# A top-32 attention with two mixtures on one core: which weight piece GpSimd subtracts, and when token and output transposes run

## The chip, the core and the metric

The kernel runs on one core of a Trainium2 chip, on TensorE (matmuls), VectorE, ScalarE, GpSimd and SyncE, each with a queue of its own that is worked off in order. SyncE's queue (SP) issues the loads, GpSimd's queue also issues the indirect transfers of the outputs. The metric is the device time of one execution in microseconds (us), the median of three runs.

## What is computed

Eight heads of attention in which each query keeps its 32 highest scores, then a dense layer with Mish, then a mixture of eight experts, of which each token takes the one with the highest cosine. The change lies in that last part:

```python
for e in range(E):                      # E = 8, D = 512, F = 1024, 1152 tokens
    mask = expert_idx == e
    h = np.maximum(x[mask] @ w1[e], 0.0)
    out[mask] = gate_w[mask, None] * (h @ w2[e])
```

## The kernel before

The attention and the dense layer come first, in an order that a planner in the file works out; the change doesn't touch it. The second mixture follows, from about 534 us to the end, in an order that is written out by hand as a loop over 64 steps (and three more): step f = 0 to 7 of expert e = 0 to 7. Tokens were sorted by expert into DRAM (`xs`), up to 176 for each expert.

All matmuls of this part are made in two parts, a high part in a shorter float format and a low part, which is the rest. So each piece of weights is split: `split_piece` (L1203) lets ScalarE copy the raw piece to the high part (L1209), and later GpSimd or VectorE subtracts the high part from the raw piece to get the low part (L1177, in the helper `low`). Which of them does it is set by the piece's number modulo 8: those in `POOL_LO` go to GpSimd, the others to VectorE. Pieces of even number are of `w1`, of odd number of `w2`, four each for an expert. Step f of expert e splits piece f of expert e + 1. There are three raw tiles of 512 KB; when a piece is subtracted, its raw tile is loaded with the piece that comes three later (`load_piece`, on SP).

A step f of expert e makes, in this order on TensorE:

- `hidden` (L1302): `phe`, the product of the tokens with 128 columns of `w1`. ScalarE and VectorE turn it into `hs` (L1315), the positive part `ht`, and its low part (L1317).
- at two of the steps, `tokens` (L1277): 4 transposes of the next expert's tokens into the one bank `pxe`/`po`, from which ScalarE (copy) and VectorE (L1177) make `xt`.
- `outputs` (L1320): the product of an earlier `ht` (three steps back) with `w2`, added up in four PSUM banks `py` 0 to 3.
- at two of the steps, `scatter` (L1355): 4 transposes of the finished outputs `yT` of the expert before into the same bank `po`; ScalarE scales them to `yo` (L1364), and GpSimd sends them out (L1365).

The outputs of expert e − 1 are finished in step 2 of expert e, and those of e begin in step 3, in the same four banks. Between the two lies `gather` (L1348): for each of the four banks ScalarE copies one half to `yT` (L1352) and VectorE adds the other half (L1353). A bank is free for the next expert when its addition is done.

Work that follows a matmul isn't put into the queues at once: `later(dt, ...)` holds it until TensorE's planned time has gone on by dt. So the order on ScalarE, VectorE, GpSimd and SP comes from the order of the steps and from these delays.

`load_tokens` loads the tokens of the expert after next (`xe`, one tile) at step 5. For the last expert (e = 7) there are no tokens to prepare, and `scatter` runs at steps 3 and 4.

Of the kernel before, what the change touches and what calls it, by code (L numbers as in the profile page):

```python
# [25 lines left out]
NE = 8  # L26
# [26 lines left out]
NRAW = 3  # L53
NIDLE = 56
NTAIL = 3
POOL_LO = (2, 5)
PE, ACT, DVE, POOL, SP = range(5)

WINDOW = 3.4133
# [255 lines left out]
def sparse_attention_mish_moe_kernel(  # L315
# [34 lines left out]
    def tp_bank(name):  # L350
        return psum.tile([P, 512], F32, tag="tp", name=name, bufs=TP[0])
# [815 lines left out]
    def later(dt, f, *a):  # L1167
        heapq.heappush(events, (clk[0] + dt, next(serial), f, a))

    def pe(dt):  # L1170
        clk[0] += dt
        while events and events[0][0] <= clk[0]:
            _, _, f, a = heapq.heappop(events)
            f(*a)
# [28 lines left out]
    def split_piece(i):  # L1203
# [5 lines left out]
        nc.scalar.activation(t[:, 0:1024], raw, AF.Copy)  # L1209
        eng = nc.gpsimd if i % 8 in POOL_LO else nc.vector  # L1210

# [9 lines left out]
    def pieces(n):  # L1221

        for _ in range(n):
            if loaded[1] < loaded[0]:
                split_piece(loaded[1])
                loaded[1] += 1
# [45 lines left out]
    def load_tokens(e):  # L1272
        xe = m2.tile([CH, 2, W], F32, tag="xe", name=f"xe{e}", bufs=1)
        nc.sync.dma_start(xe, xs[e * CAP:(e + 1) * CAP, :].rearrange("(c p) w -> p c w", p=CH))
        XE[e] = xe

    def tokens(e, d):  # L1277

        xe = XE[e]
        if d == 0:  # L1280
            XT2[e] = m2.tile([P, 4, C2], F32R, tag="xt", name=f"xt{e}", bufs=2)
            IG[e] = m2.tile([CH, 2, 2], F32, tag="ig", name=f"ig{e}", bufs=4)
            nc.gpsimd.tensor_copy(IG[e].bitcast(I32), xe[:, :, DM:W].bitcast(I32))
        xt = XT2[e]
        if e == 0 and d == 0:
            pt = psum.tile([P, 512], F32, tag="h", name=f"pxe{e}{d}", bufs=3)
        else:
            pt = tp_bank(f"pxe{e}{d}")
        for c in range(2):
            for j in range(2):  # L1290
                nc.tensor.transpose(
                    pt[:, (2 * c + j) * CH:(2 * c + j + 1) * CH],
                    xe[:, j, (2 * d + c) * P:(2 * d + c + 1) * P],
                    ident[0:CH, 0:CH],
                )
        pe(0.44)
        p3 = pt[:, 0:C2].rearrange("p (c t) -> p c t", c=2)
        hi = xt[:, 2 * d:2 * d + 2, 0:CAP]
        later(0.2, nc.scalar.activation, hi, p3, AF.Copy)
        later(0.8, low, xt[:, 2 * d:2 * d + 2, CAP:C2], p3, hi, nc.vector)  # L1300

    def hidden(e, f):  # L1302
        ph = psum.tile([P, 512], F32, tag="h", name=f"phe{e}_{f}", bufs=3)
        w = W1[e][:, f // 2].rearrange("p (l c f) -> p l c f", l=2, c=4)[:, :, :, f % 2 * P:f % 2 * P + P]
        x = XT2[e]
        for c in range(4):
            nc.tensor.matmul(ph[:, 0:C2], w[:, 0, c], x[:, c, :], start=(c == 0), stop=False)  # L1307
        for c in range(4):
            nc.tensor.matmul(ph[:, 0:CAP], w[:, 1, c], x[:, c, 0:CAP], start=False, stop=(c == 3))
        pe(1.02)  # L1310
        hs = m2.tile([P, CAP], F32, tag="hs", name=f"hs{e}_{f}", bufs=3)
        ht = m2.tile([P, C2], F32R, tag="ht", name=f"ht{e}_{f}", bufs=5)
        HT[e, f] = ht
        later(L2[0], nc.scalar.activation, hs, ph[:, CAP:C2], AF.Copy)
        later(L2[1], lambda: nc.vector.tensor_tensor(hs, hs, ph[:, 0:CAP], op=ALU.add))  # L1315
        later(L2[2], nc.scalar.activation, ht[:, 0:CAP], hs, AF.Relu)
        later(L2[3], lambda: nc.vector.scalar_tensor_tensor(  # L1317
            ht[:, CAP:C2], hs, 0.0, ht[:, 0:CAP].bitcast(F32), op0=ALU.max, op1=ALU.subtract))

    def outputs(e, f):  # L1320
        if f == 0:
            PY[e] = [psum.tile([P, 512], F32, tag=f"y{d}", name=f"py{e}_{d}", bufs=1) for d in range(4)]
        w = W2[e][:, f // 2].rearrange("p (l c d) -> p l c d", l=2, c=2)[:, :, f % 2]
        ht = HT.pop((e, f))
        for d in range(4):
            nc.tensor.matmul(PY[e][d][:, 0:C2], w[:, 0, d * P:(d + 1) * P], ht, start=(f == 0), stop=False)  # L1326
            nc.tensor.matmul(PY[e][d][:, 0:CAP], w[:, 1, d * P:(d + 1) * P], ht[:, 0:CAP], start=False, stop=(f == 7))  # L1327
            pe(0.255)
            if f == 7:
                later(0.2, gather, e, d)  # L1330

    def last_outputs(f, j):

        e = NE - 1
        if f == 0:
            PY[e, j] = psum.tile([P, 512], F32, tag=f"y{j}", name=f"py{e}_{j}", bufs=1)
        w = W2[e][:, f // 2].rearrange("p (l c d) -> p l c d", l=2, c=2)[:, :, f % 2]
        ht = HT[e, f] if j == 0 else HT.pop((e, f))
        t = slice(j * CH, j * CH + CH)
        for n, (a, l) in enumerate(((ht[:, t], 0), (ht[:, t], 1), (ht[:, CAP + j * CH:CAP + j * CH + CH], 0))):  # L1340
            nc.tensor.matmul(PY[e, j][0:CH], a, w[:, l], start=(f == 0 and n == 0), stop=(f == 7 and n == 2))
        pe(0.64)
        if f == 7:
            later(0.2, write, e, j, PY[e, j])
# [10 lines left out]
    def scatter(e, j):  # L1355
        po = tp_bank(f"po{e}{j}")
        for c in range(4):
            nc.tensor.transpose(po[0:CH, c * P:(c + 1) * P], YT[e][:, c, j * CH:(j + 1) * CH], ident)
        pe(0.44)
        later(0.2, write, e, j, po)  # L1360
# [18 lines left out]
    for g in range(8 * NE + 3):  # L1379
        e, f = g // 8, g % 8  # L1380
        if g < 8 * NE:
            hidden(e, f)
            pieces(1)
        if f in (3, 4) and e < NE - 1:
            tokens(e + 1, f - 3)
        if f == 5 and e < NE - 2:
            load_tokens(e + 2)
        if 3 <= g < 8 * NE - 5:
            outputs((g - 3) // 8, (g - 3) % 8)
        elif g >= 8 * NE - 5:  # L1390
            f_ = g - 8 * NE + 5
            last_outputs(f_, 0)
            if f_ < 8 - NTAIL:
                last_outputs(f_, 1)
        if 0 < e < NE and 0 <= f - (5 if e < NE - 1 else 3) < 2:
            scatter(e - 1, f - (5 if e < NE - 1 else 3))
    for f in range(8 - NTAIL, 8):
        last_outputs(f, 1)
    while events:
# [275 lines left out]
```

## Time and profile before

| | |
|---|---|
| three runs | 716.85, 720.65, 729.57 us, median 720.65 us |
| profiled execution | 718.75 us, of which the span from first to last instruction 717.0 us |
| busy over the span | TensorE 92%, VectorE 72%, ScalarE 71%, GpSimd 46% |
| mean granted clock of TensorE | 0.969 of full speed |
| chain that ended last, shares | TensorE 50%, transfers 15%, VectorE 14%, ScalarE 9% |

How to read the rows of the next section but one. Engines are PE (TensorE matmuls), PEld (its weight loads), DVE (VectorE), ACT (ScalarE), POOL (GpSimd), SP (SyncE). In a row of the timeline stand: start in us from the span's start, duration in us, engine, line, operation, output<-inputs, sizes and count; behind it in brackets the idle time ahead of the instruction and what ended it, where that is more than some 0.15 us. A row may hold several like instructions (x3, x4). In a row of the busy time by stretches stand: the stretch and its length, then busy us and count of PE, PEld, DVE, ACT and POOL, then the granted clock of TensorE (1.00 is full speed), the share of DMA time and GB/s. In a row of the waits: who waited, for what, us in total, how often, the longest.

### The profile page before, as it was taken

To read this page: it belongs to the slowest core of one execution; us is meant where nothing else is said; L and a number is where in the kernel's file an instruction comes from. 1 tells how busy PE (TensorE), PEld (TensorE's weight loads), DVE (VectorE), ACT (ScalarE), POOL (GpSimd) and SP (SyncE) were. 2 spreads that over 40 slices of the span, in tenths; PEclk is the share of its full clock that TensorE was granted. 3 is DMA by queue.
4 is the path that set the end of the run, shared out by engine and by line. 5 is a ranking of instruction groups with operands and counts; after the bars stand their busy time and mean duration, and the time that the engine had idled before them with its cause. 6 is when DMAs were issued, how large, how long until landed. Compare 5 with 4: busy or idle time off the path is not lost.

```text
span 717.0 us, 14819 instructions
## 1 busy us (share of the span) xinstructions
PE 659.4 (92%) x5244; PEld 500.8 (70%) x5244; DVE 519.3 (72%) x2044; ACT 506.5 (71%) x1084; POOL 332.0 (46%) x319
## 2 busy tenths in 40 slices
PE   7878788988999999999999999999989898998895
PEld 5545565655687666767667767686579898998893
DVE  4999989999987888798697783141228787778741
ACT  4868788888698877875887875773326677667651
POOL 4677786766463666344255552820013323333321
PEclk9999987999999999999999999999989999999998
DMA  9924434310012010011000001520026677777600
GB/s 257 293 93 134 146 118 142 128 43 16 30 34 49 2 32 2 3 36 39 1 1 1 31 2 60 177 88 0 0 72 224 195 229 231 226 231 225 211 24 23
DMA packets 57738, 68.98 MB, mean 96 GB/s; under 512 B 22958, under 2 KB 41390, under 8 KB 57656
## 3 DMA queue, kind: packets, MB, share of 16 engines
q1 hardware_dynamic: 55656, 63.23, 29.2%
q0 software_dynamic: 2000, 4.73, 1.9%
q8 instruction: 43, 0.70, 0.4%
q14 instruction: 39, 0.32, 0.2%
HBM read 60.32 MB, written 8.15 MB: 95 GB/s over the span
## 4 chain that ended last, share of the span: by engine, by line
PE 50%; DMA 15%; DVE 14%; ACT 9%; issue 7%; POOL 3%; POOLq 0%; SPq 0%; ACTq 0%; DVEq 0%
PE px L1054 15%; PE ph L994 12%; DMA raw<-in_moe_w_dram 8%; PE pv L885 5%; PE pt L834 4%; PE ps L673 4%; DMA out_dram<-yo,ig 2%; DVE cand L714 2%; DVE t L767 2%; PE pv L880 2%; ACT w L1209 2%; DVE w_out_s L418 1%; PE phe L1307 1%; DMA raw<-in_moe_w_in_dram 1%; ACT e L750 1%
## 5 line engine op out<-in xcount | busy, mean ns | idle before, releaser
L1054 PE MATMUL px<-w_out_s,g 128*128 128x512 f32 x288 | 142.9, 612 | 0.0
L994 PE MATMUL ph<-xT,w_in_h 128*128 128x256 f32 x576 | 90.5, 297 | 0.8 <-DVE g L1044 0.8
L1177 POOL TENSOR_TENSOR w<-raw,w 128x1024 fp32r<-128x1024 f32 x22 | 53.2, 2425 | 78.9 <-ACT w L1209 60.1
L714 DVE MAX8 cand<-sp 128x8 f32<-128x72 f32 x576 | 82.9, 217 | 2.4 <-ACT sp L441 2.3
L994 PEld LDWEIGHTS ph<-xT,w_in_h 128*128 128x128 f32 x576 | 75.0, 191 | 12.4 <-issue 5.2
L759 POOL TENSOR_SCALAR e<-sp,t 128x576 f32<-128x576 f32 x37 | 66.3, 1791 | 32.2 <-ACT e L750 26.7
L1326 PE MATMUL py<-ht,w 128*128 128x352 f32 x224 | 68.4, 364 | 11.4 <-DVE yT L1353 7.9
L1054 PEld LDWEIGHTS px<-w_out_s,g 128*128 128x128 f32 x288 | 48.3, 191 | 40.0 <-issue 36.5
L441 ACT ACTIVATE pT<-pt 128x512 f32<-128x512 f32 (+1 forms) x108 | 53.6, 519 | 27.6 <-PE pt L840 14.1
L1209 ACT ACTIVATE w<-raw 128x1024 fp32r<-128x1024 f32 x56 | 59.1, 1055 | 18.3 <-DMA raw<-in_moe_w_dram 17.8
L834 PE MATMUL pt<-ident,e 128*128 128x128 f32 (+1 forms) x360 | 58.7, 283 | 8.0 <-DVE e L807 3.9
L834 PEld LDWEIGHTS pt<-ident,e 128*128 128x128 f32 (+1 forms) x360 | 39.3, 137 | 33.0 <-issue 16.4
L773 ACT ACTIVATE e<-sp,t 128x576 f32<-128x576 f32 x72 | 54.7, 770 | 9.7 <-DVE t L767 9.3
L804 POOL TENSOR_SCALAR sp<-sp,kths 128x576 f32<-128x576 f32 x30 | 56.3, 1879 | 10.5 <-DVE t L787 8.3
L750 ACT ACTIVATE e<-sp,t 128x576 f32<-128x576 f32 x72 | 55.2, 768 | 4.9 <-POOL t L734 4.7
L1307 PE MATMUL phe<-xt,w 128*128 128x352 f32 x256 | 57.9, 351 | 0.8 <-DVE xt L1177 0.8
L767 DVE MAX8 t<-e 128x8 f32<-128x576 f32 x72 | 53.3, 750 | 6.4 <-POOL e L760 6.3
L760 POOL TENSOR_TENSOR e<-e,sp 128x576 f32<-128x576 f32 x37 | 54.3, 1467 | 3.1
L1327 PE MATMUL py<-ht,w 128*128 128x176 f32 x224 | 54.9, 245 | 0.0
L673 PE MATMUL ps<-kt,qT 64*128 64x288 f32 x256 | 49.7, 464 | 3.0 <-ACT sp L441 2.9
L441 ACT ACTIVATE sp<-ps 128x576 f32<-128x576 f32 x72 | 46.4, 644 | 8.5 <-PE ps L673 7.4
L1326 PEld LDWEIGHTS py<-ht,w 128*128 128x128 f32 x224 | 43.0, 192 | 13.3 <-DVE yT L1353 5.4
(184 smaller groups left out, 1507.9 us busy)
## 6 DMA issues: line engine op xcount, KB each, us to landing
raw<-in_moe_w_dram SPq DMA_DIRECT2D x64, 512.0 KB, 4.2
raw<-in_moe_w_in_dram SPq DMA_DIRECT2D x16, 512.0 KB, 4.6
raw<-in_moe_w_out_dram SPq DMA_DIRECT2D x16, 512.0 KB, 3.7
xs<-zt SPq DMA_DIRECT2D x11, 257.0 KB, 7.0
xe<-xs SPq DMA_DIRECT2D x8, 353.4 KB
vt<-in_v_dram SPq DMA_DIRECT2D x16, 128.0 KB, 3.2
qn<-in_q_dram SPq DMA_DIRECT2D x8, 256.0 KB, 4.2
kn<-in_k_dram SPq DMA_DIRECT2D x8, 256.0 KB, 6.2
```

Source lines behind the costliest of these rows:

```text
L441: return lambda: nc.scalar.activation(out(), in_(), func, **kw)
L673: nc.tensor.matmul(ps.tile[:, s, 0:HB], qT.tile[h], kts[0].tile[h, HB * n:HB * n + HB], start=True, stop=True)
L714: nc.vector.max(cand.tile[:, o, 8 * g:8 * g + 8], sc[o].tile[:, 72 * g:72 * g + 72])
L750: nc.scalar.activation(part(o), sc[o].tile, AF.Sign, bias=t8[:, o, 41:42], accum_out=t8[:, o, 42:43])
L759: nc.gpsimd.tensor_scalar(part(o), sc[o].tile, t8b.tile[:, o, 23:24], None, op0=ALU.is_lt)
L767: (0.67, lambda: nc.vector.max(t8b.tile[:, o, 24:32], part(o))),
L834: nc.tensor.matmul(pt.tile[0:c1 - c0, j * P:(j + 1) * P], part(o)[:, c0:c1], ident, is_transpose=True, start=(j == 0), stop=not by_pe[o], ...
L994: nc.tensor.matmul(d, a, b_, start=(m == 0), stop=(m == len(mm) - 1))
L1054: lambda f=f, f2=f2, ti=ti, x2=x2: nc.tensor.matmul(x2.tile, gt.tile[:, (f2 * n + ti) * P:(f2 * n + ti + 1) * P], w_out_s[:, f, :], start= ...
L1209: nc.scalar.activation(t[:, 0:1024], raw, AF.Copy)
L1307: nc.tensor.matmul(ph[:, 0:C2], w[:, 0, c], x[:, c, :], start=(c == 0), stop=False)
L1326: nc.tensor.matmul(PY[e][d][:, 0:C2], w[:, 0, d * P:(d + 1) * P], ht, start=(f == 0), stop=False)
```

## The change

Three numbers are changed in the hand-written order; nothing is added or taken away.

```diff
-POOL_LO = (2, 5)
+POOL_LO = (3, 5)
...
-        if f in (3, 4) and e < NE - 1:
-            tokens(e + 1, f - 3)
+        if f in (4, 5) and e < NE - 1:
+            tokens(e + 1, f - 4)
...
-        if 0 < e < NE and 0 <= f - (5 if e < NE - 1 else 3) < 2:
-            scatter(e - 1, f - (5 if e < NE - 1 else 3))
+        if 0 < e < NE and 0 <= f - (6 if e < NE - 1 else 3) < 2:
+            scatter(e - 1, f - (6 if e < NE - 1 else 3))
```

VectorE's queue at steps 2 and 3 of expert 2, before (raw_26 is the third piece of expert 3, raw_27 the fourth):

```order
L1315 TENSOR_TENSOR hs_2_7342<-hs_2_7342,phe_2_7328 128x176
L1353 TENSOR_TENSOR yT_7350<-yT_7350,py_0_7120 128x176
L1353 TENSOR_TENSOR yT_7350<-yT_7350,py_1_7121 128x176
L1353 TENSOR_TENSOR yT_7350<-yT_7350,py_2_7122 128x176
L1317 SCALAR_TENSOR_TENSOR ht_2_7343<-hs_2_7342,ht_2_7343 128x176
L1353 TENSOR_TENSOR yT_7350<-yT_7350,py_3_7123 128x176
L1315 TENSOR_TENSOR hs_3_7377<-hs_3_7377,phe_3_7360 128x176
L1177 TENSOR_TENSOR xt_7380<-pxe_7383,xt_7380 128x2x176
L1177 TENSOR_TENSOR w_3_7316<-raw_27_7311,w_3_7316 128x1024
L1317 SCALAR_TENSOR_TENSOR ht_3_7378<-hs_3_7377,ht_3_7378 128x176
```

The same place after:

```order
L1315 TENSOR_TENSOR hs_2_7342<-hs_2_7342,phe_2_7328 128x176
L1353 TENSOR_TENSOR yT_7350<-yT_7350,py_0_7110 128x176
L1353 TENSOR_TENSOR yT_7350<-yT_7350,py_1_7111 128x176
L1353 TENSOR_TENSOR yT_7350<-yT_7350,py_2_7112 128x176
L1177 TENSOR_TENSOR w_3_7288<-raw_26_7278,w_3_7288 128x1024
L1317 SCALAR_TENSOR_TENSOR ht_2_7343<-hs_2_7342,ht_2_7343 128x176
L1353 TENSOR_TENSOR yT_7350<-yT_7350,py_3_7113 128x176
L1315 TENSOR_TENSOR hs_3_7377<-hs_3_7377,phe_3_7360 128x176
L1317 SCALAR_TENSOR_TENSOR ht_3_7378<-hs_3_7377,ht_3_7378 128x176
```

The subtract of raw_26 now stands ahead of the last two instructions of the gather's place, and the subtract of raw_27 and an `xt` have left step 3.

GpSimd's queue in expert 2, one piece of the difference (`ig` are the gates and row numbers that come with the tokens):

```order
-L1177 TENSOR_TENSOR w_3_7288<-raw_26_7283,w_3_7288 128x1024
-L1283 COPY ig_7381<-xe_7186 88x4
+L1177 TENSOR_TENSOR w_3_7316<-raw_27_7311,w_3_7316 128x1024
+L1283 COPY ig_7413<-xe_7185 88x4
 L1177 TENSOR_TENSOR w_3_7316<-raw_29_7374,w_3_7316 128x1024
```

GpSimd still makes two subtracts in an expert, the fourth and the sixth piece's.

ScalarE's queue at steps 5 to 7 of expert 2, before (`raw_30` and `raw_31` are the last two pieces of expert 3, `yo` the outputs of expert 1):

```order
L1174 ACTIVATE ht_5_7454<-hs_5_7453 128x176
L1364 ACTIVATE yo_7486<-po_7468,ig_6857 88x512
L1209 ACTIVATE w_3_7288<-raw_30_7416 128x1024
L1174 ACTIVATE hs_6_7492<-phe_6_7474 128x176
L1174 ACTIVATE ht_6_7493<-hs_6_7492 128x176
L1364 ACTIVATE yo_7523<-po_7505,ig_6857 88x512
L1209 ACTIVATE w_3_7316<-raw_31_7450 128x1024
```

After, the first `yo` stands ahead of raw_31's copy and the second ahead of the copy of raw_32, the next expert's first piece, so that raw_30's copy follows `ht_5` at once. The order of the loads on SP is the same as before.

## Rows read from the trace of the kernel before

**Rows 1.** Busy time by stretches, from one T to the next, experts 2, 3, 5.

```profile
581.90:603.40 21.50, 20.29 (x153) 19.93 (x152) 16.60 (x29) 15.55 (x34) 7.86 (x5) 1.00 0.73 220
603.40:625.20 21.80, 19.54 (x136) 19.19 (x135) 16.58 (x29) 15.16 (x33) 8.00 (x5) 0.92 0.74 226
647.00:668.20 21.20, 18.71 (x141) 18.36 (x141) 16.67 (x29) 15.39 (x33) 6.98 (x5) 1.00 0.78 233
```

**Rows 2.** Waits from 534 to 702 us.

```profile
ACT w L1209 <- DMA raw<-in_moe_w_dram: 17.8, 27, 1.4
...
PE py L1326 <- DVE yT L1353: 7.9, 7, 1.3
```

**Rows 3.** The chain in order of time, 590 to 604 us (start, us, what).

```profile
590.12 5.99 DMA raw<-in_moe_w_dram
...
597.77 1.14 DVE w L1177
598.97 4.40 DMA raw<-in_moe_w_dram
```

**Rows 4.** Timeline, the gather of expert 2, from 581.8 us.

```profile
581.86 1.04 ACT L1209 ACTIVATE w<-raw 128x1024 fp32r<-128x1024 f32 x1
...
582.99 2.37 POOL L1177 TENSOR_TENSOR w<-raw,w 128x1024 fp32r<-128x1024 f32 x1 [3.83 <-DVE ht L1317]
...
583.22 0.47 PE L1291 MATMUL pxe<-ident,xe 88*128 88x88 f32 x4
583.39 0.82 DVE L1353 TENSOR_TENSOR yT<-yT,py 128x176 f32<-128x176 f32 x3
...
584.21 1.36 DVE L1317 SCALAR_TENSOR_TENSOR ht<-hs,ht 128x176 fp32r<-128x176 f32 x1
584.28 1.06 ACT L1209 ACTIVATE w<-raw 128x1024 fp32r<-128x1024 f32 x1
...
585.49 0.33 DVE L1353 TENSOR_TENSOR yT<-yT,py 128x176 f32<-128x176 f32 x1
...
585.96 0.40 PE L1326 MATMUL py<-ht,w 128*128 128x352 f32 x1 [1.12 <-ACT xt L1174]
...
586.41 1.21 DVE L1177 TENSOR_TENSOR w<-raw,w 128x1024 fp32r<-128x1024 f32 x1
...
587.55 0.33 DVE L1317 SCALAR_TENSOR_TENSOR ht<-hs,ht 128x176 fp32r<-128x176 f32 x1
```

**Rows 5.** Timeline, VectorE and GpSimd at step 5 of expert 3.

```profile
611.61 1.22 DVE L1177 TENSOR_TENSOR w<-raw,w 128x1024 fp32r<-128x1024 f32 x1
612.74 2.52 DVE L1317 SCALAR_TENSOR_TENSOR ht<-hs,ht 128x176 fp32r<-128x176 f32 x1
...
612.46 2.61 POOL L1177 TENSOR_TENSOR w<-raw,w 128x1024 fp32r<-128x1024 f32 x1 [5.26 <-ACT w L1209]
```

**Rows 6.** Timeline of ScalarE, copies of third and fourth pieces, experts 1, 3, 6.

```profile
559.59 1.06 ACT L1209 ACTIVATE w<-raw 128x1024 fp32r<-128x1024 f32 x1 [0.88 <-DMA raw<-in_moe_w_dram]
...
561.78 1.09 ACT L1209 ACTIVATE w<-raw 128x1024 fp32r<-128x1024 f32 x1
...
603.39 1.06 ACT L1209 ACTIVATE w<-raw 128x1024 fp32r<-128x1024 f32 x1 [0.56 <-DMA raw<-in_moe_w_dram]
...
606.58 1.06 ACT L1209 ACTIVATE w<-raw 128x1024 fp32r<-128x1024 f32 x1 [0.86 <-DMA raw<-in_moe_w_dram]
...
668.24 1.06 ACT L1209 ACTIVATE w<-raw 128x1024 fp32r<-128x1024 f32 x1 [0.53 <-DMA raw<-in_moe_w_dram]
...
670.65 1.06 ACT L1209 ACTIVATE w<-raw 128x1024 fp32r<-128x1024 f32 x1
```

**Rows 7.** Timeline of ScalarE at step 5 of expert 1.

```profile
571.98 0.35 ACT L1174 ACTIVATE ht<-hs 128x176 fp32r<-128x176 f32 x1 [2.31 <-DVE hs L1315]
...
572.81 1.04 ACT L1209 ACTIVATE w<-raw 128x1024 fp32r<-128x1024 f32 x1
```

## The prediction

> **What bounds the kernel now.** I looked first at the busy time by stretches. The second mixture takes the span from 534 us on, and there an expert is a period of 21 to 22 us that repeats. I count a period from T, the start of ScalarE's high-part copy of an expert's third weight piece (piece 2), because everything around the change hangs on that point. TensorE is busy for 18.7 to 20.3 us of such a period and VectorE and ScalarE for 15 to 17 us [rows 1], so no engine is full: what closes the period is a loop of waits.
>
> The waits of this stage say which. TensorE waits longest for VectorE's yT (L1353), 7.9 us in 7 places, and ScalarE waits 17.8 us for raw weight pieces [rows 2]. The chain in order of time ties them together [rows 3]: from one gather to the next it goes through a raw load of 5.99 us, a VectorE subtract, another raw load of 4.40 us, and then the ScalarE copy at 603.39 us [rows 6], which is the next T (581.86 us before it [rows 4]; period 21.53 us). Work that isn't in this loop is free as long as it stays short of it.
>
> The part of the loop that the change touches is the gather at steps 2 and 3. With T = 581.86 us, the rows [rows 4] read: GpSimd's subtract of piece 2 runs from 582.99 us for 2.37 us, up to 585.36 us. VectorE makes the first three yT additions from 583.39 us and reaches ht (L1317) at 584.21 us. That ht takes 1.36 us, while the one at 587.55 us, with GpSimd idle, takes 0.33 us. It ends at 585.57 us, 0.21 us behind GpSimd. So the yT additions, which read one operand from PSUM, run beside GpSimd's subtract, and ht, whose operands both lie in SBUF, doesn't. The fourth yT stands behind ht, starts at 585.49 us and ends at 585.82 us. TensorE, which needs the fourth py bank, goes on at 585.96 us, T + 4.10. The stall there is the one that the change could shorten.
>
> **The swap of the subtract, term 1.** In the changed order the subtract of piece 2 stands on VectorE between the third yT and ht. VectorE comes free at T + 2.35 as before. The subtract takes 1.21 us and the next instruction starts 1.14 us after it began (586.41 and 587.55 us) [rows 4], so ht starts at T + 3.49 instead of ending late at T + 3.71. It needs its plain 0.33 us, and the fourth yT starts some 0.25 us behind ht's start, at T + 3.75, and ends at T + 4.08. Before it ended at 585.82 us, T + 3.96. So a lock of 1.03 us is replaced by work of 1.14 us: about 0.13 us later, in each of the six gathers that have such a subtract beside them (experts 1 to 6): **+0.8 us**. The piece's raw tile is given back at T + 3.56 instead of T + 3.50, and the fourth piece's, now on GpSimd, about 0.2 us later than before (3.5 us behind the start of its copy where VectorE had 587.62 − 584.28 = 3.34 us [rows 4]). The fourth piece's load isn't the one that the loop in [rows 3] goes through, and the copy behind it stands in ScalarE's queue behind other work, so this is set at nothing. If it came into the loop it would be 0.2 us in six periods, 1.2 us.
>
> **Who gets GpSimd's and VectorE's common way, term 2.** GpSimd's subtract now follows the copy of the fourth piece. It asks at about 1.15 us behind that copy's start (582.99 − 581.86 = 1.13 us [rows 4]). VectorE's own subtract of piece 2 ends, and ht wants to start, at T + 3.49. If GpSimd asks earlier than that, two engines wait for the same moment. The trace shows one such meeting in full [rows 5]: VectorE's subtract from 611.61 us, GpSimd's from 612.46 us with 2.61 us where the plain one has 2.37, so it waited some 0.24 us for VectorE; then VectorE's next instruction, ht at 612.74 us, lasts 2.52 us. GpSimd, already waiting, went first, and ht paid 2.2 us. The Trainium skill's page "SBUF — State Buffer" (section "Who interferes with whom") calls this pair of ports an exclusive lock that goes to whoever issues first, for the whole instruction; it doesn't say who gets it when an instruction ends with one engine already queued, and if VectorE's next instruction went first, term 2 would be nothing. This row shows GpSimd winning, so the price stays.
>
> In which gathers does it come to this? Copy to copy, third piece to fourth, the six gathers have between 2.19 us (559.59 to 561.78 us, expert 1) and 3.19 us (603.39 to 606.58 us, expert 3), expert 6 has 2.41 us [rows 6] and expert 2 has 2.42 us (581.86 to 584.28 us) [rows 4]. The other two lie between these. Adding 1.15 us, GpSimd asks at T + 3.34 in expert 1, before ht's T + 3.49, and at T + 3.56 in experts 2 and 6, just behind it. So one gather is lost and two are close calls. A lost one makes ht end at T + 3.49 + 2.52 = T + 6.01 instead of T + 3.71: 2.3 us on the loop. I take one: **+2.3 us**. The bounds are none (0) and all six (+13.8 us).
>
> **The transposes one step later, term 3.** The two token transposes (pxe) go from steps 3 and 4 to 4 and 5, the two output transposes (po) from 5 and 6 to 6 and 7. Between two stalls TensorE does the same work as before: one pxe of 0.47 us now stands behind the stall rather than ahead of it [rows 4], and TensorE arrives at the next stall that much later, where it waits anyway (1.12 us of stall at 585.96 us). Only behind the last stall, in expert 6, nothing takes it up: **+0.45 us**. VectorE's and ScalarE's xt go to steps 4 and 5; step 5 has room, since GpSimd holds its subtract there. The token load of the expert after next keeps its place in SP's queue, right behind the raw load that the loop goes through. It waits for the second pxe, which at step 5 ends about when that raw load is issued; only the next raw load stands behind it, and that one waits for GpSimd's subtract of the sixth piece anyway. So I cost it at nothing; if the token load did hold the queue, it would be by one pxe at most, 0.47 us in six periods, 2.8 us.
>
> **The output copies, term 4.** ScalarE's yo copy of step 5 stands ahead of the seventh piece's copy. In expert 1, ht of step 5 ends at 572.33 us, and the copy starts at 572.81 us [rows 7], so 0.5 us is to be had there when yo goes a step later. It counts only in periods in which TensorE runs slowly behind the stall and ScalarE waits for it, experts 1 and 3 (the third such, expert 6, has no gather of this kind behind it): **−1.0 us**. At step 7 yo then stands ahead of the next expert's first copy, which in most experts waits for its raw piece anyway.
>
> **Sum.** The profiled execution took 718.75 us (span 717.0 us and 1.75 us around it). 718.75 + 0.8 + 2.3 + 0.45 − 1.0 = 721.3 us, that is +2.55 us. The three timed runs have their median at 720.65 us, where the same step gives 723.2 us. I take the middle, **722.3 us**.
>
> **Rivals.** *The lock is lost in most gathers.* The margin in experts 2 and 6 is under 0.1 us, and a raw piece that lands earlier moves GpSimd's request ahead of ht. It decides from a copy-to-copy distance of 2.34 us (3.49 − 1.15) downward. With four to six lost the sum is 718.75 + 0.25 + 9.2 to 13.8, so 728 to 733 us, slower than before. Against it: ScalarE waits for raw pieces in 27 places [rows 2], and where the fourth piece comes late (expert 3, 3.19 us), GpSimd asks far too late to win.
>
> *The clock stays up.* After some stalls the granted clock of the period falls: 0.92 in the period from 603.4 us, 1.00 in those from 581.9 and 647.0 us [rows 1]. Eight per cent of 21.8 us is 1.7 us, in three periods (experts 1, 3 and 6). The transposes now stand elsewhere around the stall; if TensorE's clock no longer fell, this would give back 3 x 1.7 = 5.1 us: 718.75 + 2.55 − 5.1 = 716.2 us, and 713.9 us if no gather is lost either. For it: the stall in the period from 647.0 us left the clock at 1.00, so a stall alone doesn't decide. Against it: the stall is as long as before. Turned round (clock lost in the other three) it gives 726.4 us.
>
> *The change does nothing that can be seen.* If the loop through the raw loads has a little slack that I took for none, terms 1 and 2 vanish in waits for raw pieces, and 719 to 720.5 us stand.
>
> **Chances.** My forecast (none to two gathers lost, 718 to 726 us) 0.55; most gathers lost 0.18; clock stays up, or some gain like it, 0.15; nothing seen 0.12. The low end reaches into the third case and the high end into the second: 714 to 732 us. Two per cent, about what a measurement of this kernel can tell from no change, is 14.4 us, so slower means above 735 us, for which all six gathers must be lost and the clock with them, and faster means below 706.2 us, more than all stalls that I can name here: slower 0.08, faster 0.06, same 0.86.
>
> **What would show it.** Right: in the changed trace VectorE's subtract (L1177) of 1.2 us stands between the third yT and ht, that ht has 0.33 us again, and TensorE's py goes on at T + 4.2. Term 2 shows as an ht of about 2.5 us at that place, with TensorE at T + 6.5, once or twice. ScalarE's waits for raw pieces stay near 18 us. Wrong: if TensorE goes on clearly earlier than T + 4.1, if ht is long in four or more gathers, or if the period between two T changes by more than 1 us where neither the lock nor the clock differs.

## The result: 1.3% slower in the first comparison, 0.5% in the later ones

Beside each other, four runs each, the changed kernel takes 727.9 us (723.25 to 733.49) and the kernel before 719.14 us (716.85 to 729.57): ratio 1.0134 [1.0085, 1.0182]. The time lies in the predicted range (714 to 732 us) and within 2%, but above the 718 to 726 us of the forecast's own case. Two later comparisons of the same two kernels are in the experiments: 1.0044 and 1.0051. Ratios are of the executions within 1.5% of the fastest of their kernel, medians and ranges of all, which matters for the twelve runs in experiment 1, of which four lie beyond. The profiled execution of the changed kernel took 723.25 us, of which the span 721.5 us, with TensorE busy for 92% of it at a mean granted clock of 0.960.

What the profile after shows of the second mixture, in the order of the prediction. First the waits from 534 to 705 us (who waited, for what, us in total, how often, the longest), which answer to [rows 2]:

```profile
ACT w L1209 <- DMA raw<-in_moe_w_dram: 14.4, 24, 1.4
...
PE py L1326 <- DVE yT L1353: 7.5, 6, 3.3
```

ScalarE still waits for raw weight pieces (14.4 us, before 17.8), and TensorE still waits for yT. But one of its six waits is now 3.3 us long, where the longest before was 1.3. Busy time by stretches, from T to T, experts 2 and 4 (columns as in [rows 1]):

```profile
586.30:610.80 24.50, 21.19 (x149) 20.93 (x148) 17.75 (x29) 15.09 (x32) 8.09 (x6) 0.93 0.65 202
...
632.30:654.00 21.70, 19.62 (x137) 19.27 (x136) 17.21 (x29) 15.39 (x33) 6.98 (x5) 0.92 0.75 226
```

Four of the periods of experts 1 to 5 are as long as before or shorter (20.4 to 22.0 us). Expert 2's has 24.5 us, and it is the one with the long wait. Its timeline, with T = 586.30 us (VectorE, GpSimd and TensorE; the copy of the fourth piece is at 588.51 us):

```profile
588.51 1.07 ACT L1209 ACTIVATE w<-raw 128x1024 fp32r<-128x1024 f32 x1
588.60 1.22 DVE L1177 TENSOR_TENSOR w<-raw,w 128x1024 fp32r<-128x1024 f32 x1
...
589.67 2.34 POOL L1177 TENSOR_TENSOR w<-raw,w 128x1024 fp32r<-128x1024 f32 x1 [2.53 <-ACT w L1209]
589.73 2.48 DVE L1317 SCALAR_TENSOR_TENSOR ht<-hs,ht 128x176 fp32r<-128x176 f32 x1
...
592.13 0.32 DVE L1353 TENSOR_TENSOR yT<-yT,py 128x176 f32<-128x176 f32 x1
...
592.60 0.46 PE L1326 MATMUL py<-ht,w 128*128 128x352 f32 x1 [3.31 <-DVE yT L1353]
```

This is term 2 as the prediction drew it: GpSimd asks at T + 3.37, 0.06 us ahead of ht, ht lasts 2.48 us as in [rows 5], yT ends at T + 6.15 and TensorE goes on at T + 6.30. From here on, a gather or a lock is called lost where GpSimd's subtract goes ahead of ht in this way, and the copy distance is the time from the start of the third piece's copy to that of the fourth's (here 2.21 us). The same place in expert 4, T = 632.26 us, where the fourth piece came late (copy at 635.31 us):

```profile
634.54 1.22 DVE L1177 TENSOR_TENSOR w<-raw,w 128x1024 fp32r<-128x1024 f32 x1
...
635.67 0.33 DVE L1317 SCALAR_TENSOR_TENSOR ht<-hs,ht 128x176 fp32r<-128x176 f32 x1
...
635.93 0.33 DVE L1353 TENSOR_TENSOR yT<-yT,py 128x176 f32<-128x176 f32 x1
...
636.40 0.40 PE L1326 MATMUL py<-ht,w 128*128 128x352 f32 x1 [1.16 <-ACT w L1209]
636.45 2.38 POOL L1177 TENSOR_TENSOR w<-raw,w 128x1024 fp32r<-128x1024 f32 x1 [4.38 <-ACT w L1209]
```

Here the lock is gone from the gather, as the change is made to do, and yet yT ends at T + 4.00 and TensorE goes on at T + 4.14, like before (T + 3.95 to 4.02 and T + 4.10 to 4.17). Five of the six gathers are like this one.

The profiled execution does not show 1.3%, though. Busy time by stretches, the first 125 us and the second mixture to the end (from its first `phe`), after:

```profile
0.00:125.00 125.00, 99.64 (x833) 69.39 (x833) 104.70 (x428) 92.14 (x215) 81.35 (x99) 0.88 0.55 165
...
540.30:721.50 181.20, 161.66 (x1124) 155.56 (x1124) 123.42 (x226) 114.09 (x242) 52.72 (x37) 0.95 0.59 182
```

and before:

```profile
0.00:125.00 125.00, 98.91 (x885) 69.31 (x885) 109.25 (x445) 96.51 (x225) 88.54 (x102) 0.93 0.56 168
533.90:717.00 183.10, 162.90 (x1124) 156.49 (x1124) 122.21 (x226) 113.53 (x242) 54.91 (x37) 0.94 0.59 180
```

The changed part takes 181.2 us against 183.1. It starts 6.4 us later, behind a part in which no instruction differs, and whose first 125 us had a granted clock of 0.88 instead of 0.93. The four timed executions of the changed kernel had 723.25, 724.74, 731.07 and 733.49 us at a mean granted clock of 0.960, 0.965, 0.950 and 0.949: the profiled one is the fastest, and the two longest have the lower clocks. Where those two lost theirs, no trace tells.

### The profile page after: what moved, and what is told of

It reads as the page before. It is cut to its first block, busy times and chain, and to the rows that moved or that the text cites. A ratio compares the mean times of both kernels' runs of the same rounds, so it can differ in the third digit from the quotient of the medians.

```text
span 721.5 us, 14805 instructions
## 1 busy us (share of the span) xinstructions
PE 664.1 (92%) x5244; PEld 503.5 (70%) x5244; DVE 520.6 (72%) x2044; ACT 507.6 (70%) x1084; POOL 328.5 (46%) x319
## 4 chain that ended last, share of the span: by engine, by line
PE 51%; DMA 15%; DVE 15%; ACT 8%; issue 6%; POOL 3%; POOLq 0%; SPq 0%; ACTq 0%; DVEq 0%
PE px L1054 16%; PE ph L994 12%; DMA raw<-in_moe_w_dram 8%; PE pv L885 5%; PE pt L834 5%; PE ps L673 5%; DVE cand L714 2%; DMA out_dram<-yo,ig 2%; DMA raw<-in_moe_w_out_dram 2%; PE pv L880 2%; DMA raw<-in_moe_w_in_dram 1%; DVE w_out_s L418 1%; POOL w L1177 1%; DVE w_out_s L420 1%; DVE t L767 1%
## 5 line engine op out<-in xcount | busy, mean ns | idle before, releaser
L1209 ACT ACTIVATE w<-raw 128x1024 fp32r<-128x1024 f32 x56 | 59.1, 1055 | 15.0 <-DMA raw<-in_moe_w_dram 14.4
L673 PE MATMUL ps<-kt,qT 64*128 64x288 f32 x256 | 52.0, 483 | 1.3 <-ACT sp L441 1.1
L1326 PEld LDWEIGHTS py<-ht,w 128*128 128x128 f32 x224 | 43.4, 194 | 12.7 <-ACT hs L1174 5.3
```

Of the source, the lines that this page charges most:

```text
L673: nc.tensor.matmul(ps.tile[:, s, 0:HB], qT.tile[h], kts[0].tile[h, HB * n:HB * n + HB], start=True, stop=True)
```

## Experiment 1: the same two kernels again

The changed kernel once more, the kernel before against itself, and later the changed kernel with twelve runs.

> The changed kernel once more, unaltered. In the profiled executions the second mixture (first phe to the end) took 183.1 us before and 181.2 us after, and the part ahead of it, whose instructions are the same, 533.9 and 540.3 us. Theory A (the change is worth no more than a few us; the rest of the measured difference is the part ahead, which differs from one execution to the next): ratio to before between 0.995 and 1.008, second mixture 181 to 187 us, one or two ht of about 2.5 us in the gathers. Theory B (the change costs 8 us or more in most executions, since GpSimd wins the port in most gathers, and the profiled one was a lucky one): ratio 1.010 to 1.018 again, second mixture 187 us or more with three or more long ht.

> The kernel before, unaltered, against itself, to see what the same instructions give from one execution to the next. Theory A: ratio 0.993 to 1.007, and the start of the second mixture lies anywhere from 532 to 541 us. Theory B: ratio 1.000 within 0.003 and the start at 533 to 536 us, as before.

> The changed kernel a third time, unaltered, for a narrower interval and one more trace. From the two traces so far: a gather is lost where the copy of the fourth piece starts less than about 2.3 us after the third's (2.21 and 2.19 us lost, 2.31 us not), and a lost one makes its period 24 to 25 us. Ratio 0.999 to 1.008; none to two long periods; the start of the second mixture anywhere from 534 to 541 us. If the change's loss is really the 1.3 per cent first measured: ratio 1.010 or more.

Measured: the change 1.0044 [0.9994, 1.0094] (723.66 us, six runs) and 1.0051 [1.0016, 1.0085] (726.1 us, twelve runs, 717.58 to 731.6; the kernel before 722.0 us beside it). The kernel before against itself gave 1.0039 [0.9994, 1.0083]. So a ratio can move by 0.4% with nothing changed, and of the 1.3% some 0.5% is left, +3.7 us on 722 us, and even that is little more than what the unchanged kernel shows against itself. The first `phe` stands between 533.9 and 541.4 us over all profiled executions of this study, although the part ahead of it is the same in all.

In the profiles the second mixture takes 182.5 and 181.0 us with the change and 185.0 us for the kernel before. The first of them lost the lock once (expert 3, copy distance 2.19 us, period 25.25 us), the second not at all. Such counts, one, one and none, hold for the profiled executions; two of the three are the fastest of their group, so that the mean count can be higher.

One thing these profiles do not show is the 0.5% itself: in all three of the change the second mixture, the only part in which it alters instructions, is shorter (181.2, 182.5 and 181.0 us) than in both of the kernel before (183.1 and 185.0 us). Where the timed runs spend the 3.7 us is open.

## Experiment 2: each half of the change alone

```diff
# the swap alone
-POOL_LO = (2, 5)
+POOL_LO = (3, 5)
```

> Only the subtracts swap: GpSimd the fourth instead of the third piece; transposes as before. My sum for it: 6 x 0.13 + 2.3 = +3.1 us, ratio 1.000 to 1.008, long ht in none to two gathers. If the swap is the whole loss (theory B): +8 us, ratio 1.010 or more, as much as the whole change.

```diff
# both pairs of transposes alone
-        if f in (3, 4) and e < NE - 1:
-            tokens(e + 1, f - 3)
+        if f in (4, 5) and e < NE - 1:
+            tokens(e + 1, f - 4)
...
-        if 0 < e < NE and 0 <= f - (5 if e < NE - 1 else 3) < 2:
+        if 0 < e < NE and 0 <= f - (6 if e < NE - 1 else 3) < 2:
```

> Only the transposes move by a step; GpSimd subtracts the third piece as before. My sum for it: +0.45 - 1.0 = -0.5 us, ratio 0.995 to 1.004, gather as before (ht of 1.36 us, TensorE at T + 4.1). If the transposes are the loss: +5 us or more, ratio over 1.007, with a longer period between two T.

The third kernel has only the second of these edits, the output transposes (the call of `scatter` has the same number).

> The kernel before with only the two output transposes one step later (tokens at steps 3 and 4, GpSimd on the third piece as before). My term 4 says that moving the output copies off step 5 gives the whole gain of the transposes: ratio 0.992 to 1.000, second mixture 180 to 182 us where the kernel before had 183.1 and 185.0 us, the seventh piece's copy at about T + 10.0 instead of T + 10.3 to 11.7. Rival (the tokens' step gives it): ratio 1.000 to 1.005 and 183 to 185 us.

Measured: the swap 1.0035 [0.9987, 1.0083], second mixture 185.2 us, one lost lock (expert 3, copy distance 2.18 us, ht 2.48 us). The transposes 0.9968 [0.9922, 1.0014], second mixture 180.2 us. The output transposes alone 0.9996 [0.9967, 1.0025], second mixture 183.9 us. So the measured values have the signs that were predicted, plus for the swap and minus for the transposes, but both intervals hold 1, and the intervals of the two kernels with transposes moved overlap: neither the signs nor a part of the token transposes in the minus is shown. With the output transposes alone the late copies of the seventh piece come at T + 12.1 to 12.7 where the kernel before has T + 12.8 to 13.3, not at the T + 10.0 that was expected: the 0.5 us of term 4 are there, and they bring nothing that can be measured.

## Experiment 3: take the contest away

The subtract of the third piece put behind the gather, so that neither ht nor yT waits for it:

```diff
-        later(L2[4], rest)
+        later(2.5 if i % 8 == 2 else L2[4], rest)
```

> The changed kernel with VectorE's subtract of the third piece put off until all four yT additions are in its queue (order: yT 0 to 2, ht, yT 3, subtract). If the gather is on the loop, as my prediction has it: the fourth yT ends at T + 2.9 instead of T + 4.1 or later, no ht of 2.5 us ahead of it, TensorE goes on by T + 3.1, and the second mixture is 6 x 1.2 us and one lost lock shorter, 172 to 177 us where the changed kernel had 181 and 182.5 us; ratio to before 0.985 to 0.993. Rival (the raw loads close the period anyway and the gather has slack): TensorE stalls less at the gather, but the periods stay at 21 us; ratio 0.995 to 1.003.

Its VectorE at the gather of expert 2 (T = 586.67 us):

```profile
588.22 0.82 DVE L1353 TENSOR_TENSOR yT<-yT,py 128x176 f32<-128x176 f32 x3
589.03 0.34 DVE L1317 SCALAR_TENSOR_TENSOR ht<-hs,ht 128x176 fp32r<-128x176 f32 x1
589.29 0.33 DVE L1353 TENSOR_TENSOR yT<-yT,py 128x176 f32<-128x176 f32 x1
589.54 1.22 DVE L1177 TENSOR_TENSOR w<-raw,w 128x1024 fp32r<-128x1024 f32 x1
```

The gather ends at T + 2.95 instead of T + 4.0, in all six. If it were on the loop, six periods should lose about 1 us each. Measured: 1.0041 [1.0008, 1.0074], 723.58 us, second mixture 181.5 us: nothing gained. ScalarE now waits 25.9 us for raw pieces in 36 places, where the change as it is has 14.4 to 23.1 us in 24 to 31 in its three profiles, so the microseconds seem to have gone into the loads:

```profile
ACT w L1209 <- DMA raw<-in_moe_w_dram: 25.9, 36, 1.8
```

and the chain in order of time goes through one period without touching the gather, from load to copy to load:

```profile
607.36 3.98 DMA raw<-in_moe_w_dram
...
612.51 4.33 DMA raw<-in_moe_w_dram
...
617.59 5.91 DMA raw<-in_moe_w_dram
```

By itself this run doesn't show that the gather has no part in the loop, since the raw tile of the third piece now comes free later too (T + 4.09 instead of T + 3.50), and that can eat up a gain. The third version below leaves it where it was.

The other way to take the contest away is to leave GpSimd the sixth piece alone:

```diff
-POOL_LO = (3, 5)
+POOL_LO = (5,)
```

> The changed kernel with the fourth piece's subtract on VectorE as well, so that GpSimd has only the sixth: VectorE's subtract stays in the gather, GpSimd's request is gone. Lock theory: no ht of about 2.5 us in steps 2 and 3, no period of 24 us or more, TensorE at T + 4.2 in all six gathers, second mixture 3 us shorter than the changed kernel's (178 to 180 us), ratio 0.995 to 1.000. Rival (the long periods have another cause, such as a late raw piece): one or two periods of 24 us or more remain.

Measured: 1.0023 [0.9982, 1.0063], second mixture 179.7 us, no lost gather and no period above 22.6 us, although four of the six copy distances were between 2.18 and 2.34 us, one of them (2.18 us) as short as where the lock was lost elsewhere. So the lost lock needs GpSimd's subtract; on the time the run can't be told from the change.

A third version keeps the third piece on GpSimd, moves the transposes, and puts ht behind the fourth yT:

```diff
-        later(L2[3], lambda: nc.vector.scalar_tensor_tensor(
+        later(2.6 if f == 2 else L2[3], lambda: nc.vector.scalar_tensor_tensor(
```

> Transposes one step later as in the change, GpSimd on the third piece as before, and ht of step 2 put off until the fourth yT is in VectorE's queue: the lock then falls on an ht that nobody waits for soon. If the gather is on the loop: fourth yT at T + 2.7 instead of T + 4.0, TensorE on by T + 2.9, second mixture 172 to 176 us where the transposes alone gave 180.2 us, ratio to before 0.982 to 0.992. Rival (slack in the loop): 178 to 182 us, ratio 0.995 to 1.000.

```profile
585.50 1.07 DVE L1353 TENSOR_TENSOR yT<-yT,py 128x176 f32<-128x176 f32 x4
586.50 1.21 DVE L1317 SCALAR_TENSOR_TENSOR ht<-hs,ht 128x176 fp32r<-128x176 f32 x1
```

In this timeline (expert 2, T = 583.96 us) the four additions run beside GpSimd's subtract, yT ends at T + 2.61, and ht takes the lock's wait for itself. Measured: 0.9964 [0.9934, 0.9993], 717.82 us. With the transposes alone (0.9968) it is the fastest complete version here, and it can't be told from them: of the 1.4 us in each of six gathers, 8 us, nothing that can be measured came out. Its profile has a second mixture of 178.4 us against 180.2.

## Experiment 4: double the work in the gather

If the gather has slack, adding to it shows how much. The subtract of the third piece is written twice:

```diff
+            if i % 8 == 2:
+                low(t[:, 1024:2048], raw, t[:, 0:1024], eng)
             low(t[:, 1024:2048], raw, t[:, 0:1024], eng)
```

> The changed kernel with VectorE's subtract of the third piece made twice (the same result written again), so that GpSimd's request falls into it in nearly every gather and the lock is lost each time. My price of a lost lock, 2.3 us, and of the doubled subtract, 1.14 us, says 6 x 1.14 + 5 more lost x 2.3 = +18 us against the changed kernel, 199 to 201 us of second mixture, ratio 1.02 to 1.03. If a lost lock costs 3.5 us, as the two long periods of the changed kernel (24.5 and 25.3 us against 21 to 22 us) would have it: +24 us, ratio 1.03 to 1.04. If the loop through the raw loads has slack: under +10 us.

Measured: 1.0405 [1.0347, 1.0464], 748.07 us: some 29 us more than the kernel before, where six subtracts of 1.14 us are 6.8 us. The second mixture takes 206.0 us, 25 us more than in the first profile of the change, near the +24 us that was said for a lost lock at 3.5 us. VectorE's two subtracts of expert 2 stand in one row, and GpSimd's lies between them:

```profile
588.51 4.50 DVE L1177 TENSOR_TENSOR w<-raw,w 128x1024 fp32r<-128x1024 f32 x2
```

```profile
589.58 2.35 POOL L1177 TENSOR_TENSOR w<-raw,w 128x1024 fp32r<-128x1024 f32 x1 [2.51 <-ACT w L1209]
```

yT ends at T + 7.3 to 7.6 in every expert, and the periods are 25.3 to 25.9 us instead of 20 to 23. Now the gather does set them, and ScalarE's waits for raw pieces fall to 12 (9.0 us). So an end of the gather at T + 2.6 to T + 4.0 makes no difference that can be measured, and one at T + 7.3 costs 4 us a period (25.5 us against 21.3). How much room there is beyond T + 4.0, no run shows.

## Experiment 5: take the loads out of the loop

From the twelfth piece on only one half of each raw piece is loaded; the half that isn't loaded holds old data, and everything else runs. The cut below is the load of a `w1` piece; those of `w2` are halved likewise, and the three raw tiles are fixed ones used in turn. Once with the change as it is, once with the subtract behind the gather as in experiment 3.

```diff
-            nc.sync.dma_start(raw.rearrange("p (c f) -> p c f", c=4), src)
+            n = 2 if i >= 11 else 4
+            nc.sync.dma_start(raw.rearrange("p (c f) -> p c f", c=4)[:, 0:n], src[:, 0:n])
```

> The changed kernel with 256 KB instead of 512 KB loaded for each raw piece from the twelfth on (the other half of the weights isn't loaded, the old content of the tile is split in its place), all other work the same. Putting off the subtract moved the end of the gather from T + 4.0 to T + 2.95 and left the periods at 21 to 22 us, so the loop through the raw loads, not the gather, seems to close the period as long as no lock is lost. Theory C (raw loads close it): ScalarE's waits for raw pieces nearly vanish, periods without a lost lock fall to 19 to 20 us, second mixture 170 to 175 us, though the lock may be lost in more gathers, since the fourth piece is never late; ratio 0.98 to 0.995. Rival (the gather closes it): periods stay at 21 us or more.

> The same half loads together with VectorE's subtract put off behind the gather. Theory C: with the loads out of the way the gather comes next, so here its earlier end does pay: periods of 18.9 to 19.5 us, about 1 us under those of the half loads alone and with no lost lock, second mixture 166 to 171 us, ratio 0.97 to 0.985. Rival (gather has slack against something else too): no shorter than the half loads alone where those lose no lock.

Measured: 1.0104 [1.0066, 1.0143] with the change as it is, 0.9901 [0.9871, 0.993] with the subtract moved. Half the load did not make the changed kernel any faster: in four of six gathers the fourth piece now comes early (copy distance 2.17 or 2.18 us), and exactly these four locks are lost (experts 1, 2, 3 and 5). Busy time by stretches, a period with a lost gather and the one of experts 1 to 5 without:

```profile
612.00:635.20 23.20, 20.33 (x144) 20.16 (x144) 17.81 (x29) 14.86 (x34) 8.17 (x6) 0.93 0.44 121
635.20:655.10 19.90, 19.52 (x150) 19.34 (x149) 16.76 (x29) 14.98 (x33) 7.70 (x5) 1.00 0.48 139
```

The four have 23.0 to 23.7 us, the other 19.95: a lost lock costs 3.0 to 3.7 us. With the subtract moved no gather is lost, all five periods have 20.1 us and a clock of 1.00, and the chain then passes through VectorE, from the gather to step 5, and on through TensorE without a load:

```profile
605.01 0.74 DVE yT L1357 x3
...
606.33 1.14 DVE w L1177
...
608.13 1.80 DVE ht L1321
...
611.74 2.46 DVE ht L1321
```

The two long ht are held by GpSimd's subtracts of the fourth and the sixth piece. So with whole loads it is mostly the loads that close the period, and with half loads the work of VectorE and TensorE. The earlier end of the gather brings nothing here either: 20.1 us with it, 19.95 us in the one period without a lost gather where it ends at T + 4.0. The expected 18.9 to 19.5 us and 0.97 to 0.985 were missed, and the rival (no shorter than the half loads alone where those lose no lock) held. The two kernels differ by 0.0203 of 722 us, 14.7 us, and by 11.7 us in the second mixture of their profiles (184.1 and 172.4 us); that fits four lost gathers at 2.9 to 3.7 us each.

A fourth raw tile, which would loosen the loop without leaving out work, was not run.

## What a lost lock costs, and why it is more than 2.3 us

The chain of the changed kernel in order of time passes the lost gather of expert 2, and then a second ht of the same kind:

```profile
588.68 1.14 DVE w L1177
589.81 2.39 DVE ht L1317
592.21 0.26 DVE yT L1353
...
596.88 1.13 DVE w L1177
598.01 2.45 DVE ht L1317
```

The second is step 5, where VectorE subtracts the fifth piece while GpSimd asks for the sixth: the contest of [rows 5], which the kernel before has too. Between the two TensorE ran slowly (stretches of 2.4 us, from T + 2.4 on):

```profile
588.70:591.10 2.40, 0.59 (x5) 0.38 (x3) 2.40 (x2) 1.09 (x2) 1.43 (x1) 1.00 0.53 182
591.10:593.50 2.40, 0.90 (x4) 0.93 (x5) 1.95 (x4) 0.76 (x2) 1.15 (x2) 0.85 0.85 219
593.50:595.90 2.40, 2.40 (x13) 2.40 (x12) 0.22 (x1) 0.89 (x3) 0.00 (x0) 0.50 0.62 210
```

Behind 4.8 us with 1.5 us of work the granted clock is 0.50, the lower of its two levels (1.2 GHz): 13 matmuls in a stretch where 19 to 21 fit at 1.00. The same happens behind some plain gathers. Expert 3 of the kernel before, whose T is 603.39 us:

```profile
603.40:605.80 2.40, 1.31 (x12) 1.14 (x11) 1.55 (x7) 2.32 (x7) 1.21 (x1) 1.00 0.94 302
605.80:608.20 2.40, 1.24 (x9) 1.05 (x8) 1.92 (x3) 1.62 (x3) 1.39 (x2) 0.93 0.53 181
608.20:610.60 2.40, 2.40 (x13) 2.40 (x13) 2.02 (x5) 1.61 (x3) 0.00 (x0) 0.50 0.69 207
```

and expert 2 of the same kernel, where TensorE had more to do ahead of the stall and the clock stayed up (T = 581.86 us):

```profile
581.90:584.30 2.40, 2.31 (x19) 2.14 (x18) 2.22 (x7) 2.30 (x9) 1.31 (x1) 1.00 0.57 189
584.30:586.70 2.40, 1.28 (x9) 1.09 (x9) 2.40 (x5) 1.94 (x4) 1.31 (x2) 1.00 0.70 220
586.70:589.10 2.40, 2.40 (x21) 2.40 (x20) 2.23 (x5) 1.97 (x4) 0.00 (x0) 1.00 0.65 210
```

These are the periods of experts 1 to 5 in the eleven profiles (of eight kernels) with whole loads and a single subtract, 55 in all. Where neither lock was lost (38) the mean is 21.3 us, and the clock of the period 1.00 in 33. Where only the one of step 5 was lost (14) it is 22.2 us, and the clock between 0.85 and 0.92 in 13. Where the gather's was lost (3) the step's was lost too, in the four of half loads as well; the mean of the three is 24.4 us (23.5 to 25.25), the clock 0.86 to 0.93. So a lost gather costs some 3.1 us, of which 2.1 us are the longer ht. In the three the clock falls between T + 5 and T + 7, ahead of the contest at T + 9 to T + 12, so the slow TensorE is the earlier of the two; that it causes the second loss is argued from this order and not shown by a run of its own. It can't be the whole of it: five periods kept the lock of step 5 at a lower clock, and with half loads and the subtract moved every expert lost it at a clock of 1.00.

## Why the prediction came out as it did, step by step

**The bound.** That a loop through raw loads closes most periods was right (experiments 3 and 5). The step that failed is the one that put the gather on it: "The part of the loop that the change touches is the gather". I read the chain of waits from 590 us on ([rows 3]) and took the gather ahead of it into the loop. In that period, expert 2's, the chain of the kernel before doesn't pass the gather at all: it goes from the third piece's copy through GpSimd's subtract to the next load. In the next, expert 3's, it passes the gather's ht and fourth yT:

```profile
582.99 2.37 POOL w L1177
...
585.38 3.93 DMA raw<-in_moe_w_dram
...
605.77 1.38 DVE ht L1317
607.15 0.26 DVE yT L1353
```

Of experts 1 to 5 the chain passes the fourth yT in two (1 and 3), in the second profile of the kernel before in one (2), and in the three profiles of the change in two, none and two. So a gain there is worth little (1.0 to 1.4 us earlier brought nothing that can be measured), while 2.1 us of delay were paid for with 3.1. A delay between the two was not run.

**Term 1** (+0.8 us) did not arise: yT ends at T + 3.99 to 4.02 in the gathers without a lost lock, T + 3.95 to 4.04 in the kernel before. I let VectorE's subtract start where the row of the third yT ends (T + 2.35); it starts at T + 2.28 to 2.30, since a row's end overlaps the next start by some 0.08 us, and ht at T + 3.41 to 3.43 instead of T + 3.49.

**Term 2** (+2.3 us for one lost gather) had the right mechanism, with one, one and none in three profiles. That the count came out as said is partly luck: expert 1, which was to be lost, had a copy distance of 2.43 us in the first profile of the change and kept its lock, and expert 2, a "close call", lost it at 2.21 us. The raw pieces land at other times in every execution. Two sizes were off. The price is 3.1 us and not 2.3, since clock and step 5 follow. And the threshold is a copy distance of about 2.2 us and not 2.34: losses came at 2.17 to 2.21 us, 2.19 us was lost once and went well twice, and from 2.30 us on none was lost. For this the place of ht counts (T + 3.43), and that GpSimd has to be ahead by some margin. At the distances read before (2.42 and 2.41 us) the "close calls" of experts 2 and 6 would have been none, and the rival "lost in most gathers", which I gave 0.18, needs pieces that land earlier than they do; in experiment 5 they do, and it came true there with four. The later return of the fourth piece's tile was set at nothing because the loop doesn't go through its load; in the second profile of the change the chain does go through it once (expert 2: GpSimd's subtract of 2.38 us from 591.07 us, then a load of 4.59 us), so that up to 1.2 us, as the prediction priced it, may be there.

**Terms 3 and 4** (+0.45 and −1.0, together −0.55 us) are neither confirmed nor refuted: the transposes alone give 0.9968 [0.9922, 1.0014], which holds both −0.55 us (0.9992) and no change; their second mixture, in one profile, is 2.9 us shorter than the 183.1 us of the kernel before. The reason given for the late copies of the seventh piece was too short. "TensorE runs slowly" holds, but between it and the copy stands the lock of step 5: the copy is at T + 12.06 or later in all 14 periods in which that was lost, at T + 9.7 to 12.0 in the 38 others. With both pairs of transposes moved, fewer periods of these profiles lose it (one of five in the transposes alone, none with yT first, two or three of five in the kernel before and with the output transposes alone); with the whole change it is one to three, the lost gathers among them. Whether the token transposes bring that about, and how, is open.

**The sum.** +2.55 us was predicted and +3.7 us [1.2 to 6.1] is the narrowest measurement. That they agree isn't a proof of the terms, and for the size it is luck: term 1 did not arise, term 2 costs more for each lost gather, terms 3 and 4 can't be told from nothing, and the profiles, in which the changed part is shorter than before, don't show where 3.7 us are spent. The kernel with the subtract behind the gather loses no gather and measures 1.0041 [1.0008, 1.0074], the same. What it shares with the change, and not with the two faster versions, is VectorE subtracting the third piece; but so does the kernel with the sixth piece alone on GpSimd, at 1.0023 [0.9982, 1.0063]. With the subtract behind the gather the raw tile comes free at T + 4.09 (589.54 + 1.22 us) instead of T + 3.50, 0.59 us in six gathers, 3.5 us if all of it is on the load loop; this is an estimate from those rows. In the change itself the tile comes free at T + 3.50 (634.54 + 1.22 us), as before, so this doesn't account for its +0.5%. Lost gathers at 3.1 us each can be a part of that; the rest is open.

**The rivals.** "Nothing seen" came nearer than its 0.12: the narrowest measurement is little more than the kernel before shows against itself, and a gather that ends early brings nothing. "The clock stays up" can't be confirmed; the periods at a lower clock are three of five in the first profile of the change, one of five in each of the two others, two of five in the two of the kernel before. Its price was too high: 0.9 us separates periods with and without a lost lock at step 5, where I had taken 1.7.

**What would show it.** The marks for the swap came as said: ht has 0.33 us again, TensorE goes on at T + 4.14 to 4.16 (4.2 was said), behind a lost lock at T + 6.30 (6.5). ScalarE's waits for raw pieces, said to stay near 18 us, were 14.4, 18.0 and 23.1 us in the three profiles. One of the other marks was no good: a period that changes by more than 1 us with neither lock nor clock behind it happens in both kernels (23.37 us in the kernel before, 22.77 us in the change, both at a clock of 1.00 with no lost lock). So a mark of 1 us in a single period can't tell the kernels apart.

## What to carry over

Before an engine's wait is priced in full, it is to be shown that the period hangs on it: one kernel with the piece earlier and one with it later (here 1 us earlier gave nothing, 3.3 us later cost 4 us a period) says more than the chain of one period. Where a subtract of GpSimd holds up an instruction of VectorE, as it does ht here and not yT, it belongs where VectorE's next instruction reads PSUM or where nobody waits for it; a copy that starts 0.1 us earlier (2.21 instead of 2.30 us) cost 3 us. And a half per cent on a kernel that gives 1.0039 against itself is not settled by a dozen runs on each side.

## What the runs showed of the hardware

Who goes first when VectorE passes from its subtract to ht turns on a few hundredths of a microsecond. In six of the seven lost gathers (leaving out the kernel with the doubled subtract) GpSimd's row starts 0.06 or 0.07 us ahead of ht's. In the seventh, in the kernel with half loads, expert 1, it starts 0.03 us ahead and also goes first:

```profile
568.22 2.51 DVE L1321 SCALAR_TENSOR_TENSOR ht<-hs,ht 128x176 fp32r<-128x176 f32 x1
```

```profile
568.19 2.34 POOL L1177 TENSOR_TENSOR w<-raw,w 128x1024 fp32r<-128x1024 f32 x1 [11.79 <-ACT w L1213]
```

In the third profile of the change, expert 1, it starts 0.02 us ahead and has to wait (2.60 us instead of 2.38), while ht has its 0.33:

```profile
564.47 0.33 DVE L1317 SCALAR_TENSOR_TENSOR ht<-hs,ht 128x176 fp32r<-128x176 f32 x1
```

```profile
564.45 2.60 POOL L1177 TENSOR_TENSOR w<-raw,w 128x1024 fp32r<-128x1024 f32 x1 [14.39 <-ACT w L1209]
```

The Trainium skill's page "SBUF — State Buffer" (section "Who interferes with whom") says that issue order decides who blocks, and that a VectorE instruction with at most one operand in SBUF, outside the modes that use two ports, doesn't contend. The traces agree with the second: yT, with one operand in PSUM, takes 1.07 us for four beside GpSimd's subtract. For the first, the six leads of 0.06 and 0.07 us agree, ht being held for GpSimd's whole subtract; at 0.02 and 0.03 us the starts in the rows don't tell who will go first, and which moment decides there is open.

The other surprise is the part that nothing changed: it ends between 533.9 and 541.4 us in the fourteen profiled executions, with a granted clock of 0.88 to 0.93 in its first 125 us. The four that end earliest (533.9 to 536.0 us) have 0.93 there, the four that end latest (540.3 to 541.4 us) 0.88 or 0.89. What makes that clock differ is open.
